# Windowed attention and a gated convolution layer on one core: decoding two weight parts at once, the smaller half of x by TensorE in two units, score bursts next to each other, and a new written-out order

## The chip, the cores and the metric

One core of a Trainium2 chip. The time is that of one execution in microseconds (us) on the device; lower is better. Three runs of the kernel before are given, and one more execution was profiled.

## What is computed

For 8 sequences of 576 positions, 8 heads of 64:

```python
scores = scale * np.matmul(q, k.transpose(0, 1, 3, 2))
mask = (rel >= 0) & (rel < window)            # window 64
attn = softmax of the masked scores
x = attention output, laid out as (batch, seq, 512)
h = np.maximum(x @ w_in, 0.0)                 # 512 -> 1024
conv_out += conv_w[k][None, None, :] * hp[:, k:k + S, :]   # 3 taps along seq
gate = 1.0 / (1.0 + np.exp(-conv_out))
return (h * gate @ w_out)                     # 1024 -> 512
```

The weights come as 64-bit floats, and the kernel decodes them on the chip.

## The kernel before, in words

The 4,608 positions are cut into 12 units of 384. A unit's **attention** has 12 tiles of 64 queries, in bursts: six bursts of two tiles in units 0 and 1, three bursts of four tiles in the others. For a burst TensorE makes the scores (`scores`, L538), VectorE adds the mask and takes the row's extreme (`row_max`, L559), ScalarE takes the exponential (`exps`, L569), and after `guard` and `reciprocal` VectorE or GpSimd normalises (`normalise`, L588). In units 0 and 1 TensorE turns the result (`turn`, L595) and ScalarE or VectorE copies it back (`unturn`, L600); in the others VectorE transposes blocks (L607) and DMAs place them (`place`, L620). `values` (L627) multiplies by v. Its result in PSUM is split in a larger half `xh` (`split_hi`, L632) and the rest `xl` (`split_lo`, L637, always VectorE), so that products of the fp32r kind keep their accuracy.

A unit's **layer** has 8 parts f of 128 hidden columns: `mm1` (L644, 12 matmuls of 384 columns: larger and smaller half of w_in against xh, larger half against xl), `relu` (L670 or L672), for each pair of parts the convolution (`conv_mid` L686 or L688, two `conv_side` L693), `sigmoid` (L697), `gate` (L704), `gate_hi` (L709), `gate_lo` (L714), and `mm2` (L723, 3 matmuls of 512 columns for each part and 128 rows; L728 in the last unit). `result` and the stores follow.

Sixteen weight parts (8 of w_in, 8 of w_out, 512 columns each) are **decoded**: `load_w`, `magnitude` (L438 or L440), `shift` (L444), `sign` (L448), `low` (L451, ScalarE), `add_low` (L455), then `larger` (L471) and `lo` (L475) make the two fp32r halves. Before, only `shift` works on two parts at once.

The PSUM has eight banks. The table gives `scores` a bank for the first head and takes the next one for the second head, so a burst holds two; `mm2` sums in banks 4 to 6, and 0, 1 and 7 go to `mm1` and `values` in turn. TensorE runs `mm1` and `mm2` on fp32r operands and `scores`, `turn` and `values` on fp32 operands.

`plan()` lists the pieces of work, and the string `ORDER` names them one by one: a number is a piece, `/4` its first bank, A, D or P the engine where there is a choice (ScalarE, VectorE, GpSimd), and `F5/0` five `fill` matmuls (L404) on a tile of zeros whose result nobody reads. The instructions are issued in this order, and each engine runs its own in that order.

Of the kernel before, what the change touches and what calls it, by code (L numbers as in the profile page):

```python
# [15 lines left out]
P = 128  # L16
# [21 lines left out]


# [83 lines left out]
def plan():  # L123
# [63 lines left out]
    at("identity")  # L187
    for m in (1, 2):
        at("later_masks", m)
# [60 lines left out]
    224P 240 93P 151A 77/1 231 225 70 152P 75D 232 76 213 78D 226P 468 79 146A 316 73 199 242 215P 233P 206 82  # L250
    F5/2 94/0 147D 241 207P 249 119A 234 120D 123 243P 216 83 121 208/4 250 105/1 122 251 235D 252A 209A 217D
    469 84 128 127 153/7 168 317A 244 200 85 253 245P 96D 318A 106D 107A 254D 3 321 227/5 108 110A 218/6 319
    236/4 155A 111 219A 255/0 326 109 473/2 228A 112 470 246/1 256A 325 367 113 260/7 346 124 169 129 257/0 396
    125P 474 237A 258D 114P 247A 259 261A 475 F3/6 263/1 158A 477 262 266/0 270 320 484/2 327 126D 156/7 264A
    633 322 267A 345 115A 328D 323P 265 170A 268 116P 130A 485 269/1 174 486 157A 161A 131D 179 159 509/2 479
    329D 133/5 171A 324D 634 271A 162 272/0 366 476 172 472 487 173 178 478 290/7 175 273A 480D 163 490 274D 488
    275 136 481 635 160 277A 397 293/1 482P 510 489 471 511 176A 491A 512 278 134/6 177P 492 483 164 132/4 180
    495 137 279 639/2 372 636 165D 369A 135 520 276 166A 330/0 493D 181A 280 167D 513 182P 640 183 508 185 291
    494 281P 186 292D 368A 501 188 641 351 500 184 514 370 507 187 294A 376 502 282A 650/2 371 505 295A 283P
    333/7 504 515 652 499 191A 651 498 190A 797 373 516A 189A 286/6 503 517 518D 374A 285/5 496 348A 375P 519  # L260
    497 288 377 289 298A 332D 523 546 656 674/2 296 506 334A 297 284/4 522 653 299 381/1 378 347A 798 525 300
    356 335D 530 379A 349 301 532 380D 536/0 531 338D 287 355 521 675 528 384/7 383A 302P 537A 526 676 654 524
    538 527 421/1 303D 529 304D 644 799 350 678 336 305 385A 386D 677 306 339 352 533/0 645 340 542/7 655 389D
    337 307 534A 357 643 308 387 800 657A 341 358P 535 309 543D 353P 310 544 424/0 390 642 342D 354D 442/7 422
    658 391 423A 659D 343A 425A 388 646A 539/1 679 344D 445/0 398A 540D 680 647 541 648P 312A 673 681A 392 545/1
    682 359D 683P 649 429A 361/5 660 547A 364 402 393D 661 399A 814/2 638 567 684 311A 662 443 548/1 313A 663
    400 394A 690 401 667 403 668 430 360/4 549A 406 671 363 444A 395D 426A 637 566/1 407 427 404A 428 687 431
    688 569/7 408 192 405D 409A 691 815 446A 410P 686 432 412 664 568A 447D 411 694 450A 433P 816 817 696 362/6
    314 587/0 669 451 588 434D 689 448 414 666 452 590/1 672 435D 695 553D 550A 554 693 417A 415 551 692 449 365
    685 418A 555 413 570A 670 591A 838/2 820 665 437/5 453 839 440 840 416 552 436/4 454D 556 439 419D 818 803/2  # L270
    557D 438/6 961 455D 441 456D 843 697/7 558D 574A 706/1 805 698A 819 459 699 707D 589A 462 821P 559P 808 804
# [12 lines left out]
    767 991 1142/2 917A 885P 992 902A 770 1000 899A 1144 995 788 990 903 769 1143 993 768 989 900 787 999 904
    1166/2 1024 901 918/1 1014 905 1167 966 886A 994 632 1146 887P 771 919D 791 1168 790 1145 906P 789 1172
    1131/2 1170 792 1289 923A 1025/7 793A 795D 1028/0 1133 936/1 907D 1137 908P 1026A 920A 1027 1148 888/4 1029D
    938D 1290 1147 1034/7 1030 1136 1031/1 924 1149P 1171 891 925 1038 1150 1035D 941A 939/0 1059 1132 1151P
    1169 1134 921 909 794A 1291 940D 1032A 890/6 1135 1173D 942 889/5 944D 1138A 892 922 1036 893 926 1165 911
    1139 1033 914 943 1037/0 945 1292 1174 946 1175D 1040/7 1140D 927D 1058/1 1176 928A 1039A 1183 929D 1184
    1061/0 1042D 1060A 1141 947 1152 1041A 948P 932 1157 1306/2 1182 1161 1079/1 1043 1164 1101 949D 1179 1080  # L290
    1308 1187 950D 910 1130 1312 1186 913 1044 1160 912 1307 1163 935 1062A 1045D 1153 1063D 1081A 1330/2 1064
    1185 1066A 1046 953 1311 796 1188 1067 931 1331 934 1047 1180 956 1332 1048 1181 930 1068 1177 952 1065 1159
    933 1155 1069 951 1049P 1158 959A 1295/2 1154 1082/7 1297 1202 1050A 1162 1178 1333 1051D 1453 954 1129
    1084D 1156 1085 1054/6 1336 1070D 1057 1309 1100/0 1296 1083A 1071D 957A 1072P 1334 955 1299 1454 1052/4
    1310 1103/1 1223 1087A 1313P 1335 1088 1102A 1089 1055 958A 1298 1198/7 1104A 1195/0 1455 1199D 1301 1192/1
    1200 1105A 1086 1189/7 1193A 1106 1196A 1075 1314 1300 1108D 1197 1053/5 1302A 1090 1303 1056 1194 1304P
    1190D 1073 1191 1456 1074 1294 1337A 1315P 1305 1078 1076 1201/0 1091P 1316 1329 1327 1320 1109 1092A 1077
    1338 1339D 1204/1 1093P 1340 1352 1470/2 1344 1244 1222/7 1347 1471 1349 1107 1324 1472 1319 1096 1203D
    1224A 1326 1099 1110 1351 1206D 1494/2 1111 1207 1318 1225/7 1208 1474 1343 1496 1348 1112D 1325 1293 1476
    1094 1113D 1317 1226D 1097 1473 1114P 1322 1495 1095 1350 1205D 1243/0 1209A 1230D 1499 1231 1210 1498  # L300
    1459/2 1227D 1475 1228 1246/7 1617 1232 1245A 1328 1477D 1229 1321 1478 1211 1233 960 1115 1479P 1460 1341
# [58 lines left out]
def attention_moe(ctx: ExitStack, tc: tile.TileContext, q, k, v, first, w_in, conv_w, w_out, out):  # L360
# [96 lines left out]
    def part(buf, j):  # L457
        return wx[buf][:, j * DM:(j + 1) * DM]
# [391 lines left out]
```

## Time and profile before

| | |
|---|---|
| time, median of 3 runs | 514.66 us (514.45 to 516.1) |
| the profiled execution | 513.32 us, span 511.5 us |
| TensorE, matmuls | 499.8 us busy (98%) |
| VectorE | 398.7 us (78%) |
| ScalarE | 327.1 us (64%) |
| GpSimd | 169.2 us (33%) |

PE is TensorE's matmuls, PEld its weight loads, DVE is VectorE, ACT ScalarE, POOL GpSimd, SP the queue that issues DMAs. Matmuls overlap, so a matmul's own duration is longer than the step from one to the next, and PE busy is not PE at its peak; the chain view gives the steps. The chain that ended last is 87% TensorE and 9% VectorE by the page.

### The profile page before, as it was taken

The page shows a single profiled execution, that of the slowest core. Times are in us where ns is not written, and L with a number is a line of the kernel's source. Part 1 is how long each engine was busy: PE and PEld are TensorE (multiplying, and loading weights), DVE is VectorE, ACT ScalarE, POOL GpSimd, SP SyncE. Part 2 cuts the span into 40 slices and gives each one's busy share as a digit, 9 for nine tenths or more (in the row PEclk, how much of TensorE's full clock was granted, in tenths as well). Part 3 has the DMA queues.
Part 4 walks back from the last instruction along what each step waited for, and adds up shares of the span by engine and source line. Part 5 has one row for each costly group of instructions (what it writes and reads, how often), then busy time and mean ns, then how long its engine had stood idle before and what let it go on. Part 6 is the DMA issues. An engine that isn't in the chain of part 4 may idle for free.

```text
span 511.5 us, 13953 instructions
## 1 busy us (share of the span) xinstructions
PE 499.8 (98%) x5375; PEld 438.2 (86%) x5375; DVE 398.7 (78%) x1197; ACT 327.1 (64%) x923; POOL 169.2 (33%) x254
## 2 busy tenths in 40 slices
PE   8798999999999999999999999999999999999997
PEld 5587978998888898898888889988889889898996
DVE  5999999997996986597667858887386778846682
ACT  5999999967837863855864874572792675242330
POOL 6766452430441442511332532121344131152020
PEclk9999999999999999999999999999999999999999
DMA  8996635082634533804642613806263303410011
GB/s 326 405 408 216 257 84 146 6 288 85 161 104 114 175 70 105 261 4 125 212 144 70 219 62 112 258 14 197 59 254 110 108 13 113 124 62 33 0 63 62
DMA packets 27570, 71.98 MB, mean 141 GB/s; under 512 B 5744, under 2 KB 14064, under 8 KB 27504
## 3 DMA queue, kind: packets, MB, share of 16 engines
q1 hardware_dynamic: 27216, 69.52, 40.8%
q0 software_dynamic: 288, 1.57, 1.8%
q8 instruction: 42, 0.69, 0.6%
q14 instruction: 24, 0.20, 0.1%
HBM read 48.26 MB, written 11.01 MB: 116 GB/s over the span
## 4 chain that ended last, share of the span: by engine, by line
PE 87%; DVE 9%; POOL 2%; issue 1%; ACT 0%; POOLq 0%
PE bank L723 36%; PE bank L644 36%; PE bank L627 7%; PE bank L538 5%; PE bank L728 3%; DVE s L559 2%; DVE c L693 1%; DVE wx L448 1%; DVE xl L637 1%; POOL s L588 1%; DVE wx L455 1%; DVE s L588 1%; DVE wx L444 0%; ACT s L569 0%; POOL mask L493 0%
## 5 line engine op out<-in xcount | busy, mean ns | idle before, releaser
L644 PE MATMUL bank<-xh,w_in 128*128 128x384 f32 x768 | 197.5, 338 | 0.0
L723 PE MATMUL bank<-w_out,gh 128*128 128x512 f32 x528 | 168.8, 401 | 0.0
L644 PEld LDWEIGHTS bank<-xh,w_in 128*128 128x128 f32 x768 | 138.8, 188 | 7.0
L693 DVE SCALAR_TENSOR_TENSOR c<-hbuf,cw,c 128x386 f32<-128x386 f32 (+1 forms) x192 | 125.0, 674 | 13.8 <-ACT c L686 12.5
L644 PE MATMUL bank<-xl,w_in 128*128 128x384 f32 x384 | 129.0, 336 | 0.9 <-DVE xl L637 0.9
L569 ACT ACTIVATE s<-s,nm 128x96 f32<-128x96 f32 (+2 forms) x288 | 105.2, 368 | 17.1 <-DVE nm L559 16.9
L723 PEld LDWEIGHTS bank<-w_out,gh 128*128 128x128 f32 x528 | 96.0, 188 | 19.0 <-POOL w_out L475 0.2
L723 PE MATMUL bank<-w_out,gl 128*128 128x512 f32 x264 | 104.2, 395 | 0.2 <-DVE gl L714 0.2
L704 POOL TENSOR_TENSOR c<-c,hbuf 128x386 f32<-128x386 f32 (+5 forms) x39 | 44.8, 1166 | 110.4 <-ACT c L697 110.4
L559 DVE CUSTOM_DVE_ANT_0 s<-bank,mask 128x96 f32<-128x96 f32 (+2 forms) x288 | 56.6, 255 | 29.3 <-PE bank L538 25.1
L644 PEld LDWEIGHTS bank<-xl,w_in 128*128 128x128 f32 x384 | 72.1, 188 | 1.3 <-DVE xl L637 1.3
L697 ACT ACTIVATE c<-c 128x772 f32<-128x772 f32 (+1 forms) x48 | 40.6, 849 | 35.6 <-DVE c L693 35.3
L714 POOL TENSOR_TENSOR gl<-c,gh 128x768 fp32r<-128x768 f32 (+1 forms) x22 | 42.5, 1930 | 57.5 <-DVE gh L709 32.0
L723 PEld LDWEIGHTS bank<-w_out,gl 128*128 128x128 f32 x264 | 49.5, 188 | 12.2 <-DVE gl L714 0.6
L569 ACT ACTIVATION_READ_ACCUMULATOR s<-s,nm 128x1 f32 x288 | 54.6, 189 | 0.0
L670 ACT ACTIVATE hbuf<-bank 128x384 f32<-128x384 f32 x55 | 26.0, 484 | 44.1 <-PE bank L644 41.8
L588 POOL TENSOR_TENSOR s<-s,r 128x768 f32<-128x768 f32 (+1 forms) x22 | 30.1, 1376 | 62.0 <-DVE r L581 57.8
L686 ACT ACTIVATE c<-hbuf,cw 128x386 f32<-128x386 f32 (+1 forms) x57 | 34.1, 613 | 17.2 <-POOL gl L714 6.4
L627 PEld LDWEIGHTS bank<-ub,v 128*64 128x64 f32 x1152 | 35.6, 138 | 8.2 <-issue 4.4
L538 PEld LDWEIGHTS bank<-qk 64*32 64x32 f32 (+1 forms) x2112 | 29.6, 110 | 13.3 <-issue 6.6
L627 PE MATMUL bank<-ub,v 128*64 128x64 f32 x1152 | 38.7, 224 | 1.3 <-ACT ub L600 1.3
L538 PE MATMUL bank<-qk 64*32 64x96 f32 (+2 forms) x2112 | 38.2, 253 | 1.0 <-DMA qk<-in_first_dram 0.6
(78 smaller groups left out, 538.0 us busy)
## 6 DMA issues: line engine op xcount, KB each, us to landing
v<-in_v_dram SPq DMA_DIRECT2D x24, 768.0 KB, 5.5
ub<-T SPq DMA_DIRECT2D x240, 48.0 KB, 2.2
qk<-in_k_dram SPq DMA_DIRECT2D x20, 448.0 KB, 4.6
out_dram<-ot SPq DMA_DIRECT2D x11, 768.0 KB, 4.7
qk<-in_q_dram SPq DMA_DIRECT2D x20, 384.0 KB, 5.5
raw_in<-in_w_in_dram SPq DMA_DIRECT2D x8, 512.0 KB, 6.3
raw_out<-in_w_out_dram SPq DMA_DIRECT2D x8, 512.0 KB, 7.7
qk<-in_first_dram SPq DMA_DIRECT2D x12, 320.0 KB, 4.6
```

Source lines behind the costliest of these rows:

```text
L538: nc.tensor.matmul(banks[bank[h]][r:r + rows, i * P + o:i * P + k], qq[hs, s:s + rows], kk[hs, s + o:s + k], start=True, stop=True)
L559: nc.vector.tensor_tensor_reduce(out=ss[n // NB][:, n % NB, h, o:k], in0=banks[bank[h]][:, i * P + o:i * P + k], in1=mask[m][:, o:k], scal ...
L569: nc.scalar.activation(x, x, AF.Exp, bias=small(nms, (n,))[:, h:h + 1], scale=-1.0, accum_out=small(sms, (n,))[:, h:h + 1])
L588: engine[on].tensor_tensor(sv, sv, small(rs, ns).unsqueeze(2).broadcast_to([P, 2 * len(ns), k]), ALU.mult)
L627: nc.tensor.matmul(banks[bank[0]][h * D:(h + 1) * D, t * W:(t + 1) * W], vs[:, c, t, h], ub[g][:, 2 * p:2 * p + 2, 2 * t + h], start=True, ...
L644: nc.tensor.matmul(banks[bank[0]][:, :NX], w[:, a, c], y[x][:, c], start=(c == 0 and j == 0), stop=(c == NC - 1 and j == 2))
L686: nc.scalar.activation(c, h, AF.Copy, scale=w)
L693: nc.vector.scalar_tensor_tensor(c, h, w, c, op0=ALU.mult, op1=ALU.add)
L697: nc.scalar.activation(both(u, j), both(u, j), AF.Sigmoid)
L704: engine[on].tensor_tensor(c[:, :, a:a + n], c[:, :, a + o:a + o + n], h[:, :, 1 + a + o:1 + a + o + n], ALU.mult)
L714: engine[on].tensor_tensor(gls[j % 3][:, :, :n], cs[j % 2][:, :, :n], ghs[j % 3][:, :, :n].bitcast(F32), ALU.subtract)
L723: nc.tensor.matmul(banks[bank[0]], x, wts["out", f][:, w], start=(start and i == 0), stop=(stop and i == 2))
```

## The change

- All of a decode step's instructions now take a whole pair of parts (1,024 columns) where the pair belongs together, which is the case for 14 of the 16 parts; the raw tile and the weight tile of a pair are one tile each.
- In units 1 and 2 the smaller half of x is made by TensorE: `less` adds minus `xh` to the result of `values` in the same bank (one matmul of 384 columns against a negated identity, built once by `minus`), and `split_rest` copies the rest out on ScalarE (5 times) or VectorE (3 times). `split_lo` stays in the other units.
- `values` starts its bank only with its first tile.
- `ORDER` is another one, with 12 `fill` matmuls in place of 23. It also moves work between engines.

```diff
+BY_DIFFERENCE = (1, 2)
...
-        for j, f in enumerate(fs):
-            at("magnitude", key, f, buf, j)
-        at("shift", key, fs, buf)
-        for j, f in enumerate(fs):
-            for fn in ("sign", "low", "add_low", "larger", "lo"):
-                at(fn, key, f, buf, j)
+        for fn in ("magnitude", "shift", "sign", "low", "add_low", "larger", "lo"):
+            at(fn, key, fs, buf)
...
             at("values", u, c, bank=bank)
             at("split_hi", u, c, bank=bank)
-            at("split_lo", u, c, bank=bank)
+            if u in BY_DIFFERENCE:
+                at("less", u, c, bank=bank)
+                at("split_rest", u, c, bank=bank)
+            else:
+                at("split_lo", u, c, bank=bank)
...
-    2 6 8 5 97 4 86 7 13 41 9 0 F5/0 31/2 50/4 382 95 32 195 1 22/6 80 331 154 51 33 98D 23 F3/0 12/2 99 34 100
+    0 7 98 5 9 143 351 8 1 6 42 2 312 10 14 F4/0 32/2 33 178 102 87 99D 34 F3/0 13/4 100 101 51/6 103 176 15 133
...
-    def part(buf, j):
-        return wx[buf][:, j * DM:(j + 1) * DM]
+    def part(buf, fs):
+        return wx[buf][:, :len(fs) * DM]
...
+        w = wts[key, fs] = pool.tile([P, 2, len(fs) * DM], F32R, name=f"w_{key}{fs[0]}", tag=f"{key}{fs[0]}")
+        for j, f in enumerate(fs):
+            wts[key, f] = w[:, :, j * DM:(j + 1) * DM]
+        copy(on)(w[:, 0], part(buf, fs))
...
+    def minus():
+        nc.scalar.activation(negated, ident, AF.Copy, scale=-1.0)
...
-                                 ub[g][:, 2 * p:2 * p + 2, 2 * t + h], start=True, stop=True)
+                                 ub[g][:, 2 * p:2 * p + 2, 2 * t + h], start=(t == 0), stop=(t == NT - 1))
...
+    def less(u, c, bank):
+        nc.tensor.matmul(banks[bank[0]][:, :NX], negated, xh[x_of(u)][:, c], start=False, stop=True,
+                         skip_group_check=True)
...
+    def split_rest(u, c, on, bank):
+        copy(on)(xl[x_of(u)][:, c], banks[bank[0]][:, :NX])
```

Three places of the order. **GpSimd at the start**: mask_75 is the mask that the scores of units 0 and 1 need, mask_76 a mask of the later units. Before, from the program's first mask on:

```order
L489 MEMSET mask_76 128x128
L493 ISA
L493 AFFINE_SELECT mask_76<-mask_76 32x96
L495 AFFINE_SELECT mask_76<-mask_76 32x96
...
L551 MEMSET s_81 128x2x64
L551 MEMSET s_82 128x2x64
L489 MEMSET mask_75 128x128
L493 AFFINE_SELECT mask_75<-mask_75 64x128
L495 AFFINE_SELECT mask_75<-mask_75 64x128
L493 AFFINE_SELECT mask_75<-mask_75 64x128
L495 AFFINE_SELECT mask_75<-mask_75 64x128
```

Now:

```order
L497 MEMSET mask_75 128x128
L501 ISA
L501 AFFINE_SELECT mask_75<-mask_75 64x128
L503 AFFINE_SELECT mask_75<-mask_75 64x128
L501 AFFINE_SELECT mask_75<-mask_75 64x128
L503 AFFINE_SELECT mask_75<-mask_75 64x128
L674 MEMSET hbuf 128x2x2
```

The mask that is needed first is now made first; the ten instructions for the other mask and the two blanks no longer stand ahead of it.

**TensorE at the values of unit 1** (ub_61 and ub_62 hold the two groups of turned weights; before, bank_104 is bank 0, now bank_105 is). Before:

```order
L595 MATMUL bank_105<-ident,s_83 128x128 x4
L627 MATMUL bank_111<-ub_61,v 64x64 x12
L627 MATMUL bank_104<-ub_61,v 64x64 x12
L404 MATMUL bank_110<-spare 128x512 x3
L627 MATMUL bank_105<-ub_62,v 64x64 x12
L627 MATMUL bank_104<-ub_62,v 64x64 x12
L538 MATMUL bank_106<-qk 32x96
```

Now, with `less` on L653 (negated is the negated identity):

```order
L639 MATMUL bank_106<-ub_61,v 64x64 x12
L639 MATMUL bank_105<-ub_61,v 64x64 x12
L607 MATMUL bank_111<-ident,s_83 128x128 x4
L653 MATMUL bank_106<-xh_64,negated 128x384
L665 MATMUL bank_112<-xh_63,w_in_459 128x384 x2
...
L639 MATMUL bank_106<-ub_62,v 64x64 x12
L639 MATMUL bank_112<-ub_62,v 64x64 x12
L653 MATMUL bank_105<-xh_64,negated 128x384
L653 MATMUL bank_106<-xh_64,negated 128x384
L550 MATMUL bank_107<-qk 32x96
```

Each bank of values gets one matmul more; three fills are gone; and an `mm1` stands between the two halves of the values.

**TensorE at the scores of unit 7**, now: two bursts stand next to each other, the first in banks 2 and 3 (bank_107, bank_108), the second in banks 0 and 1 (bank_105, bank_106). Before, the three bursts of this unit stand apart, with `mm1` and `mm2` between them, all three in banks 2 and 3.

```order
L744 MATMUL bank_110<-w_out_1376,gl_99 128x512
L550 MATMUL bank_107<-qk 32x96
L550 MATMUL bank_108<-qk 32x96
...
L550 MATMUL bank_107<-qk 32x96
L550 MATMUL bank_108<-qk 32x96
L550 MATMUL bank_105<-qk 32x96
L550 MATMUL bank_106<-qk 32x96
...
L550 MATMUL bank_105<-qk 32x96
L550 MATMUL bank_106<-qk 32x96
L744 MATMUL bank_110<-w_out_1376,gh_96 128x512 x2
```

This is so in units 7 to 11; over the whole order, TensorE's stretches of fp32 work (scores, turns, values) between fp32r work go from 54 to 48.

## Rows read from the trace of the kernel before

**Rows 1.** The page: TensorE's busy time, and its busy tenths in 40 slices of the span.

```profile
PE 499.8 (98%) x5375; PEld 438.2 (86%) x5375; DVE 398.7 (78%) x1197; ACT 327.1 (64%) x923; POOL 169.2 (33%) x254
...
PE   8798999999999999999999999999999999999997
```

**Rows 2.** Stretches of the span (us): length, busy time of each engine with its instructions, then TensorE's granted clock (1.00 is the full one), the DMA engines' share, and GB/s.

```profile
6.00:9.00 3.00, 2.89 (x37) 1.84 (x30) 2.97 (x23) 2.77 (x13) 0.49 (x7) 1.00 1.02 402
...
30.00:45.00 15.00, 13.57 (x277) 12.11 (x278) 14.93 (x52) 14.91 (x35) 9.78 (x21) 1.00 0.76 304
45.00:70.00 25.00, 24.84 (x326) 21.42 (x307) 24.90 (x86) 24.04 (x72) 12.23 (x13) 1.00 0.57 202
70.00:98.00 28.00, 28.00 (x280) 25.01 (x281) 27.29 (x79) 27.87 (x85) 9.08 (x11) 1.00 0.36 100
98.00:300.00 202.00, 202.00 (x2242) 176.56 (x2242) 160.74 (x478) 132.78 (x373) 64.29 (x84) 1.00 0.46 139
300.00:508.00 208.00, 207.93 (x1937) 185.90 (x1935) 146.29 (x380) 103.29 (x263) 52.57 (x73) 1.00 0.30 95
```

**Rows 3.** What TensorE's matmuls waited for in the first 70 us: total us, times, the longest.

```profile
PE bank L595 <- POOL s L588: 3.1, 4, 1.2
...
PE bank L627 <- ACT ub L600: 1.3, 1, 1.3
PE bank L644 <- DVE xl L637: 0.9, 1, 0.9
...
PE bank L723 <- DVE gl L714: 0.2, 1, 0.2
```

**Rows 4.** The chain that ended last, from 60 to 80 us: start, us, what.

```profile
64.15 0.88 DVE gl L714
65.03 0.04 issue
65.08 3.97 PE bank L723 x16
```

**Rows 5.** In order of time, the start: GpSimd's masks, VectorE's first work on scores, TensorE's first scores. Start, duration, engine, line, what, and idle time before it.

```profile
0.73 0.20 POOL L489 MEMSET mask<- 128x128 f32 x1 [0.29 <-POOLq L839]
...
3.84 0.20 POOL L489 MEMSET mask<- 128x128 f32 x1
...
3.88 2.84 PE L538 MATMUL bank<-qk 64*64 64x128 f32 x48
...
5.16 0.29 POOL L495 TENSOR_SCALAR_AFFINE_SELECT mask<-mask 64x128 f32<-64x128 f32 x1
...
5.48 0.29 DVE L559 CUSTOM_DVE_ANT_0 s<-bank,mask 128x128 f32<-128x128 f32 x1 [4.09 <-POOL mask L495]
```

**Rows 6.** Groups by line and shape in the first 70 us: instructions, busy us, mean ns of one, idle time before.

```profile
L448 DVE SCALAR_TENSOR_TENSOR wx<-raw_in,wx 128x512 uint32<-128x512 uint32 x8 | 5.4, 691 | 0.1
L451 ACT ACTIVATE raw_in<-raw_in 128x512 uint32<-128x512 uint32 x7 | 4.8, 680 | 0.0
L637 DVE TENSOR_TENSOR xl<-bank,xh 128x384 fp32r<-128x384 f32 x8 | 4.2, 549 | 0.1
L475 POOL TENSOR_TENSOR w_in<-wx,w_in 128x512 fp32r<-128x512 f32 x3 | 4.2, 1418 | 0.1
L444 DVE TENSOR_SCALAR wx<-wx 128x1024 uint32<-128x1024 uint32 x5 | 3.8, 751 | 0.1
L632 ACT CAST xh<-bank 128x384 fp32r<-128x384 f32 x5 | 2.2, 475 | 0.0
L475 DVE TENSOR_TENSOR w_in<-wx,w_in 128x512 fp32r<-128x512 f32 x3 | 2.0, 681 | 0.0
L714 POOL TENSOR_TENSOR gl<-c,gh 128x768 fp32r<-128x768 f32 x1 | 1.9, 1859 | 0.0
L714 DVE TENSOR_TENSOR gl<-c,gh 128x768 fp32r<-128x768 f32 x1 | 0.9, 949 | 0.0
L444 DVE TENSOR_SCALAR wx<-wx 128x512 uint32<-128x512 uint32 x2 | 0.8, 418 | 0.0
```

**Rows 7.** In order of time, VectorE and GpSimd between 56 and 60 us (columns as in the rows 5).

```profile
56.18 0.57 DVE L693 SCALAR_TENSOR_TENSOR c<-hbuf,cw,c 128x386 f32<-128x386 f32 x1
...
58.04 1.29 POOL L475 TENSOR_TENSOR w_out<-wx,w_out 128x512 fp32r<-128x512 f32 x1
...
58.09 1.67 DVE L693 SCALAR_TENSOR_TENSOR c<-hbuf,cw,c 128x386 f32<-128x386 f32 x1
```

**Rows 8.** The chain that ended last, later pieces: start, us, what, number of matmuls.

```profile
76.00 0.90 PE bank L723 x3
...
102.58 2.31 PE bank L644 x12
...
112.53 2.11 PE bank L644 x12
114.64 0.71 PE bank L723 x3
...
126.70 1.55 PE bank L627 x48
...
259.12 3.02 PE bank L627 x96
```

**Rows 9.** In order of time, two groups of fills on TensorE.

```profile
1.45 2.50 PE L404 MATMUL bank<-spare 128*128 128x512 f32 x5 [1.45 <-DVE spare L760]
...
40.48 0.96 PE L404 MATMUL bank<-spare 128*128 128x512 f32 x3
```

More of the change, by code (lines that the diff above doesn't have):

```diff
@@ L250 @@
[L250 to L259, printed above, removed]
@@ new lines @@
+    944 845A 844A 955 752A 846 959 848A 753P 715 991 863A 963 716 987 735 847 966 864/7 849 962 980 956 1109/2
+    865D 986 869A 882/0 965 1111 960 866D 850 964 1110 851 958 885/1 870 985 867 983 868 961 871 733 932 872 957
+    1133/2 1113 967 873P 736 1135 988 754 984 1134 734 852P 990 1112 737 886A 884A 1098/2 1139 1026 1005 738
+    1136 904 1100 1256 1138 903/7 853D 1099 1114 854P 755 905A 1115 890D 756 874D 1257 757 891 875P 759 760A
+    1104 758 855/4 1137 858 1116A 1101 1117 1118P 998/1 1258 1103 1001/0 762A 999D 908A 1000 992/7 887D 888
@@ new lines @@
+    1227 1482 1338 1606 1477 1229 1244D 1355A 1626 1452 1605 1590/2 1627 1425 1607 1356/7 1480 1339 1630 1473
+    1608D 1342 1479 1245D 1459 1225 1358D 1357A 1455 1343 1230 1361D 1472 1362 1247 1359 1424 1374/0 1609 1453
+    1591 1344P 1748 1457 1481 1228 1363 1345A 1248 1497 1360 1250 1346P 1376D 1364 1377/1 1631 1365P 1749 1246
+    1476 1628 1251 1253A 1379D 1395/7 1396 1592 1254A 1518 1593 1610D 1629 1380 1249 1632D 1633 1378D 1634P
+    1349/6 1252A 1596 1348/5 1255 1381 1750 1484/0 1382A 1383 1487/1 1485A 1595 1486 1347/4 1488D 1594 1352
@@ L345 @@
+    2070D 2051 2071D 2031 2056 2030 2049 2050 2054 2073 2077 2055 2075 2079 2074 2088 2086 2082D 2053 2089 2083
+    2078 2087 2072 2084D 2076 2085 2080A 2081
 """
@@ L379, in attention_moe @@
     ident = pool.tile([P, P], F32, name="ident")
+    negated = pool.tile([P, P], F32R, name="negated")
     qk = pool.tile([P, FIRST], F32, name="qk")
@@ L424, in load_w @@
     def load_w(key, f):
-        raws[key, f] = pool.tile([P, DM, 2], U32, name=f"raw_{key}{f}", tag=f"{key}{f}")
-        nc.sync.dma_start(raws[key, f].rearrange("p e two -> p (e two)"), src[key][f].bitcast(U32))
+        fs = next(fs for k, fs in DECODE if k == key and f in fs)
+        if (key, fs) not in raws:
+            raws[key, fs] = pool.tile([P, len(fs) * DM, 2], U32, name=f"raw_{key}{fs[0]}", tag=f"{key}{fs[0]}")
+        a = fs.index(f) * DM
+        nc.sync.dma_start(raws[key, fs][:, a:a + DM].rearrange("p e two -> p (e two)"), src[key][f].bitcast(U32))
     @work
@@ L455, in to_add_low @@
         nc.vector.tensor_tensor(xu, xu, lw, ALU.add)
-    def part(buf, j):
-        return wx[buf][:, j * DM:(j + 1) * DM]
-    fn["magnitude"] = lambda key, f, buf, j, on: to_magnitude(part(buf, j), raws[key, f][..., 1], on)
-    fn["sign"] = lambda key, f, buf, j: to_sign(part(buf, j), raws[key, f][..., 1])
-    fn["low"] = lambda key, f, buf, j: to_low(raws[key, f][..., 0])
-    fn["add_low"] = lambda key, f, buf, j: to_add_low(part(buf, j), raws[key, f][..., 0])
+    def part(buf, fs):
+        return wx[buf][:, :len(fs) * DM]
+    fn["magnitude"] = lambda key, fs, buf, on: to_magnitude(part(buf, fs), raws[key, fs][..., 1], on)
+    fn["sign"] = lambda key, fs, buf: to_sign(part(buf, fs), raws[key, fs][..., 1])
+    fn["low"] = lambda key, fs, buf: to_low(raws[key, fs][..., 0])
+    fn["add_low"] = lambda key, fs, buf: to_add_low(part(buf, fs), raws[key, fs][..., 0])
     def copy(on):
@@ L468, in larger, with lo @@
     @work
-    def larger(key, f, buf, j, on):
-        wts[key, f] = pool.tile([P, 2, DM], F32R, name=f"w_{key}{f}", tag=f"{key}{f}")
-        copy(on)(wts[key, f][:, 0], part(buf, j))
+    def larger(key, fs, buf, on):
+        w = wts[key, fs] = pool.tile([P, 2, len(fs) * DM], F32R, name=f"w_{key}{fs[0]}", tag=f"{key}{fs[0]}")
+        for j, f in enumerate(fs):
+            wts[key, f] = w[:, :, j * DM:(j + 1) * DM]
+        copy(on)(w[:, 0], part(buf, fs))
     @work
-    def lo(key, f, buf, j, on):
-        engine[on].tensor_tensor(wts[key, f][:, 1], part(buf, j), wts[key, f][:, 0].bitcast(F32), ALU.subtract)
+    def lo(key, fs, buf, on):
+        w = wts[key, fs]
+        engine[on].tensor_tensor(w[:, 1], part(buf, fs), w[:, 0].bitcast(F32), ALU.subtract)
     @work
@@ L506, in identity @@
         make_identity(nc, ident)
+    @work
+    def minus():
+        nc.scalar.activation(negated, ident, AF.Copy, scale=-1.0)
     @work
@@ L637, in split_lo @@
         nc.vector.tensor_tensor(xl[x][:, c], banks[bank[0]][:, :NX], xh[x][:, c].bitcast(F32), ALU.subtract)
+    @work
+    def less(u, c, bank):
+        nc.tensor.matmul(banks[bank[0]][:, :NX], negated, xh[x_of(u)][:, c], start=False, stop=True,
+                         skip_group_check=True)
+    @work
+    def split_rest(u, c, on, bank):
+        copy(on)(xl[x_of(u)][:, c], banks[bank[0]][:, :NX])
     @work
```

175 lines of the change are left out of this document (86 added, 89 removed).

## The prediction

> **What bounds the kernel now.** I read the page first: TensorE is busy 98% of the span, and only the first tenth of it shows gaps [rows 1]. Then the stretches: from 70 us to 508 us its matmuls fill 437.93 of 438 us at the full granted clock, and the view of what they waited for has no entry after 70 us [rows 2]. Up to 70 us it is different. VectorE is busy 14.93 of 15 us and 24.90 of 25 us, ScalarE 14.91 and 24.04, while TensorE stands in some places for normalised scores (3.1 us), a copied bank (1.3), the smaller half of x (0.9) and a last time for the smaller half of the gate (0.2) [rows 2, 3]. That last one is where the chain leaves VectorE: gate_lo ends and TensorE starts at 65.08 us and is never released by anyone again [rows 4]. So the time is: when TensorE becomes dense, plus the work that it has left then. A microsecond is won in the first 70 us only through VectorE and ScalarE, and later only by less work on TensorE.
>
> **The change, part by part.** The sum is made against the profiled execution, 513.32 us, which lies 1.34 us under the median of 514.66 us; the difference found is then taken from the median. I counted each engine's work in both orders up to the same piece of TensorE work, at the step from one instruction to the next: on VectorE a row's mean less about 0.08 us of overlap, on ScalarE less about 0.1.
>
> *Start.* VectorE's first row_max waits 4.09 us for the mask, which ends at 5.45 us, since another mask is made first, from 0.73 to 3.84 us [rows 5]. With its own mask first (five instructions, 1.6 us from the second memset to the end), the mask is ready near 2.4 us. Late next are the scores: TensorE starts them at 3.88 us, 48 in 2.84 us, so 16 of a burst take 0.95 us and VectorE can start at 4.9 instead of 5.48 us. Gain 0.6 us; between 0 (the second burst's data now land behind a weight part) and 1.3 (if ScalarE wins as well).
>
> *Up to the fourth mm1 of unit 0* (29 us of TensorE work, 45 us in the trace) VectorE has 38.1 us to do in place of 38.3, ScalarE 37.3 in place of 37.2, GpSimd 25.3 in place of 28.5. Pairing is worth little: two halves of 512 columns are 836 ns, one of 1,024 is 751, so 0.08 us for each of the 22 or so instructions saved on VectorE and some 0.13 on ScalarE, estimated the same way [rows 6]. And part of the pairs is not yet due. I take 0.2 us gained, between 1.0 gained and 0.5 lost.
>
> *less.* Eight matmuls of 384 columns at 2.11 / 12 = 0.176 us [rows 8] are 1.4 us on TensorE. Four belong to unit 1, where TensorE waits anyway (the 1.3 us for the bank copied by ScalarE stand right between the two halves of these values) [rows 3]; I let them cost 0.1. The four of unit 2 lie where it is dense and cost 0.7. Sum 0.8; bounds 0.7 and 1.4. split_lo in return frees VectorE of eight times 0.47 us [rows 6]; three copies of the same length come back there, and five of 0.37 go to ScalarE. Both are in the loads here and below.
>
> *Between 29 and 76 us of TensorE work* the new order shifts work off GpSimd. By 76 us VectorE has lo (+2.1 us, now as pairs), two more gates (+1.9), two more gate_lo (+1.7), two more normalise (+1.5) and magnitudes (+1.1), and loses split_lo (-2.4 net of copies), a few conv_mid (-1.0) and relu (-0.9), and unturn, sign and add_low (-1.4), with small things of +0.4: +3.0. ScalarE gets +0.9, GpSimd -12.8 (lo 4.0, gate 3.6, gate_lo 3.6, normalise 1.0). VectorE had no idle time there, so this is the danger. What eases it is that a VectorE instruction with two inputs in SBUF waits out a GpSimd one: the convolution that takes 0.57 us took 1.67 when a GpSimd lo of 1.29 began 0.05 us earlier [rows 7]. Between 45 and 98 us VectorE is busy 52.2 us [rows 2], and its instructions there at their usual steps are some 49.3 us by my count, so some 2.9 us are such waiting; with half of GpSimd's work I expect half of that back, 1.4. So VectorE is later by 3.0 - 0.8 (the gains above) - 1.4 = 0.8 us. TensorE itself is later by 0.8 + 0.2 (less, and one more switch, below) - 0.8 = 0.2, so VectorE loses 0.6 against it, and by how much its results lay ready the trace does not tell. I take 0.2 us lost; bounds 0 and 3.
>
> *Switches.* Behind scores or values the next mm1 takes 2.31 us in place of 2.11, the next three mm2 matmuls 0.90 in place of 0.71, and two separate pairs of values take 2 x 1.55 where four in one go take 3.02 [rows 8]. A stretch of fp32 work thus costs 0.20 to 0.28 us beyond its matmuls; I take 0.24. After 80 us of TensorE work the order has 32 of them in place of 38, by bursts next to each other and by values in threes: 1.4 us gained (1.2 to 1.7). In the middle there is one more: 0.2 lost.
>
> *Fills.* Eleven fewer. The ones removed stand in waits, so I cost them at nothing; that cover is the wait itself, and if it is gone a fill less is a gain. [...]
>
> The *end* (results and stores of the last unit) keeps its shape, cost nothing. Sum: -0.6 - 0.2 + 0.8 + 0.2 - 1.4 + 0.2 = **-1.0 us**: 512.3 for the profiled execution, **513.7 us** as a median. Some 0.3% (1.5 us) is what a measurement can tell from no change here, so this is inside it, on the fast side.
>
> **Rivals.** *(1) More of it counts.* The start gives 1.0, the first stage 0.5, less costs 0.7, VectorE is no later, switches give 1.7 and take 0.2: -2.3 us, 512.4. For it speaks that TensorE has no wait after 70 us even though VectorE is just as full up to 98 us [rows 2], so results lie ready. *(2) VectorE becomes the bound between 65 and 120 us (slower).* If GpSimd's relief does not come and the results were only just ready, the 3.0 us count in full, and less 1.2: -0.6 - 0.2 + 1.2 + 3.0 + 0.2 - 1.4 = +2.2, 516.9. It decides the sign once TensorE waits more than 1.2 us for gate_lo, xl or relu there. The 0.2 us wait at 65 us [rows 3, 4] says that this slack can be gone. *(3) The bursts do not stay next to each other in effect.* Two bursts hold four banks, and the third needs the first two back; if VectorE is late with the row_max, TensorE waits in five units, up to 0.5 us each: +1.5, 516.2. Against it: a second burst (0.93 us) and two mm2 groups (1.4 us) stand between in the closest place, and VectorE has idle time in that part (160.74 of 202 us) [rows 2]. [...]
>
> **How the numbers follow.** Forecast 0.45; rival 1 0.35; rival 2 0.12; rival 3 0.04; rival 4 0.04. The forecast's own bounds run from about -1.9 to +0.7 by terms that do not all fall to one side. The range takes in rival 1 with some 0.5 us below it and most of the way to rival 2: 511.9 to 516.4. Faster by over 0.3% (under 513.1): rival 1 and a little of the forecast, 0.37. Within: most of the forecast and a part of the rivals at the border, 0.44. Slower: rivals 2 to 4, 0.19.
>
> **What would show it.** Right: VectorE's first row_max near 4.9 us; the fourth mm1 of unit 0 starts at 44 to 45 us; no matmul wait after 70 us beyond 0.5 us; three mm2 matmuls behind two bursts still 0.90, with six such stretches fewer; less near 0.18 us each. Wrong: TensorE waiting for VectorE between 65 and 120 us (rival 2), waits of scores for nm at units 7 to 11 (rival 3), a granted clock under 1.00 (rival 4), or a start of the dense part later than 66 us.

## The result and the profile after

520.0 us as a median (518.13 to 520.15), against 514.62 for the kernel before on the same chip: 1.0083 times as long, 95% interval 1.0061 to 1.0105. The forecast was 513.7 and its range ended at 516.4; the change makes the kernel slower by 5.4 us. The profiled execution took 520.15 us against 513.32 before, 6.8 us more; their spans, 518.1 and 511.5 us, are 6.6 apart. (The execution profiled before lay 1.3 us under its median, which is why these are more than 5.4.)

The page shows where to look. TensorE's busy time grew by only 1.0 us, its tenths show a new dent in the 22nd slice (272 to 285 us), and the granted clock, shown full in all slices before, is lower in the third and in that 22nd:

```profile
PE 500.8 (97%) x5372; PEld 441.5 (85%) x5372; DVE 399.9 (77%) x1186; ACT 321.8 (62%) x905; POOL 156.7 (30%) x238
...
PE   8679999999999999999997999999999999999997
...
PEclk9989999999999999999998999999999999999999
...
q8 instruction: 42, 0.69, 0.6%
```

What the matmuls waited for, over the whole run (before, the main rows are those of [rows 3]):

```profile
PE bank L607 <- POOL s L600: 5.1, 2, 3.5
PE bank L550 <- issue: 3.0, 1, 3.0
PE bank L639 <- ACT ub L612: 1.8, 2, 1.0
PE bank L406 <- DVE spare L781: 1.5, 1, 1.5
PE bank L550 <- DMA qk<-in_first_dram: 1.1, 4, 0.3
PE bank L607 <- DVE s L600: 0.9, 2, 0.6
PE bank L639 <- DVE nm L571: 0.5, 1, 0.5
```

Two rows are new: one wait of 3.5 us for GpSimd's normalise, and one of 3.0 us for "issue", that is for nothing that the profile knows. The first begins at 28 us. The second stands in the chain at 278.86 us, in the middle of a burst of scores; it is called the standstill from here on:

```profile
274.85 1.67 PE bank L550 x99
276.52 1.59 PE bank L744 x6
278.12 0.74 PE bank L550 x43
278.86 3.00 issue
281.86 0.66 PE bank L550 x18
282.52 1.57 PE bank L744 x3
284.09 2.77 PE bank L665 x12
```

Behind it three mm2 matmuls take 1.57 us and an mm1 2.77, where 0.71 (0.90 behind a burst) and 2.11 are usual [rows 8]. The stretches that answer to [rows 2]:

```profile
30.00:45.00 15.00, 12.96 (x170) 12.18 (x171) 14.04 (x42) 11.62 (x32) 10.95 (x15) 0.89 0.82 328
45.00:70.00 25.00, 25.00 (x347) 22.31 (x346) 24.93 (x66) 24.82 (x59) 7.45 (x10) 1.00 0.60 215
70.00:98.00 28.00, 28.00 (x316) 23.88 (x314) 27.72 (x86) 27.60 (x90) 4.74 (x7) 1.00 0.45 135
98.00:300.00 202.00, 199.00 (x2207) 175.13 (x2207) 155.93 (x472) 129.06 (x360) 62.99 (x88) 0.99 0.45 133
300.00:508.00 208.00, 208.00 (x1979) 186.37 (x1978) 151.91 (x395) 103.79 (x268) 52.33 (x70) 1.00 0.31 96
```

From 45 us on TensorE is full but for the 3.0 us. From 30 to 45 it is less full than before (12.96 against 13.57 us), and VectorE, which had next to no idle time there before, now has 1.0 us.

To place the loss I worked out from the matmul records how much TensorE is behind: the start of a matmul less the usual steps of all matmuls ahead of it (0.174 us for 384 columns, 0.233 for 512, 0.109 for a turn, 0.033 for one of values, 0.015 to 0.017 of scores; fills count as nothing). In us, at these times of the span:

```
                        20 us   50 us   80 us  270 us  300 us     end
before                  15.48   22.30   23.66   27.30   28.06   30.48
after                   15.61   25.25   25.86   29.36   34.34   35.79
e3_mask_early           15.75   22.90   23.51   27.02   31.46   32.99
e5_unit8_apart          15.48   25.28   25.85   29.31   29.87   31.45
e6_data_later           15.62   25.33   25.87   29.34   30.12   31.63
e7_mask_early_unit8...  15.39   22.58   23.15   26.48   27.05   28.67
```

Before to after: +0.13 up to 20 us, +2.82 from there to 50, -0.89 to 270, +4.22 in the 30 us of the standstill, -0.97 behind it; the eight `less` matmuls add 1.39 us of steps. Together this is +6.7, the difference of the spans (6.6) but for rounding. So there are two losses, 2.8 and 4.2 us, and a gain of some 1.9 us outside them, where the forecast had one.

### The profile page after: what moved, and what is told of

Its sections match the earlier page's. It is cut to its first block, busy times and chain, and to the rows that moved or that the text cites. A ratio compares the mean times of both kernels' runs of the same rounds, so it can differ in the third digit from the quotient of the medians.

```text
span 518.1 us, 13893 instructions
## 1 busy us (share of the span) xinstructions
PE 500.8 (97%) x5372; PEld 441.5 (85%) x5372; DVE 399.9 (77%) x1186; ACT 321.8 (62%) x905; POOL 156.7 (30%) x238
## 3 DMA queue, kind: packets, MB, share of 16 engines
q0 software_dynamic: 288, 1.57, 1.7%
## 4 chain that ended last, share of the span: by engine, by line
PE 93%; DMA 2%; issue 1%; DVE 1%; ACT 1%; POOL 0%; SPq 0%
PE bank L665 40%; PE bank L744 37%; PE bank L639 7%; PE bank L550 6%; PE bank L749 3%; DMA qk<-in_first_dram 2%; PE bank L607 1%; PE bank L653 0%; ACT s L581 0%; DVE s L571 0%; DVE wx L460 0%; POOL s L600 0%; POOL w_in L478 0%; SPq L411 0%; DVE w_in L483 0%
## 5 line engine op out<-in xcount | busy, mean ns | idle before, releaser
L665 PEld LDWEIGHTS bank<-xh,w_in 128*128 128x128 f32 x768 | 140.6, 190 | 6.2
L714 DVE SCALAR_TENSOR_TENSOR c<-hbuf,cw,c 128x386 f32<-128x386 f32 (+1 forms) x192 | 120.6, 655 | 14.7 <-ACT c L707 13.0
L735 POOL TENSOR_TENSOR gl<-c,gh 128x768 fp32r<-128x768 f32 x21 | 39.8, 1894 | 92.6 <-ACT gh L730 56.1
L725 POOL TENSOR_TENSOR c<-c,hbuf 128x386 f32<-128x386 f32 (+5 forms) x31 | 37.8, 1237 | 79.1 <-ACT c L718 79.1
L707 ACT ACTIVATE c<-hbuf,cw 128x386 f32<-128x386 f32 (+1 forms) x59 | 35.4, 614 | 30.9 <-DVE hbuf L693 24.1
L639 PEld LDWEIGHTS bank<-ub,v 128*64 128x64 f32 x1152 | 35.7, 138 | 9.1 <-issue 5.3
L693 DVE TENSOR_SCALAR hbuf<-bank 128x384 f32<-128x384 f32 x40 | 21.8, 549 | 26.9 <-PE bank L665 25.7
```

What stands on the lines that cost most here:

```text
L639: nc.tensor.matmul(banks[bank[0]][h * D:(h + 1) * D, t * W:(t + 1) * W], vs[:, c, t, h], ub[g][:, 2 * p:2 * p + 2, 2 * t + h], start=(t == ...
L665: nc.tensor.matmul(banks[bank[0]][:, :NX], w[:, a, c], y[x][:, c], start=(c == 0 and j == 0), stop=(c == NC - 1 and j == 2))
L707: nc.scalar.activation(c, h, AF.Copy, scale=w)
L714: nc.vector.scalar_tensor_tensor(c, h, w, c, op0=ALU.mult, op1=ALU.add)
L725: engine[on].tensor_tensor(c[:, :, a:a + n], c[:, :, a + o:a + o + n], h[:, :, 1 + a + o:1 + a + o + n], ALU.mult)
L735: engine[on].tensor_tensor(gls[j % 3][:, :, :n], cs[j % 2][:, :, :n], ghs[j % 3][:, :, :n].bitcast(F32), ALU.subtract)
```

## The experiments

All times are medians; the kernel before ran beside them (514.64, 514.73 and 515.19 us in the three sets). In these kernels' traces the line numbers are two lower, since the table of numbers wraps differently (in the second experiment two higher). In the diffs a token is a step of the table, a number and behind a slash its bank: 4 and 3 are the masks of later units, 1437/2 and 1426/2 the first and third burst of unit 8, 1171/0 an mm1, 1260 the load of v, 927 the store, 1584 a load of k.

**First: the third burst moved, at the wrong unit.** Theory A: TensorE runs out of instructions, since scores and their weight loads use them up at some 140 per us (64 of each in the 0.93 us of a burst).

```diff
-1262/2
 1097 1298 1148 1046/7
+1262/2
```

> The changed kernel with one edit: the third burst of unit 7 (scores(7,0)) stands behind mm1(5,4) instead of in front of it, so that 24 slow instructions (2.1 us) stand between the double burst and it. Theory A (TensorE ran out of instructions at 278.6 us: 384 scores and their weight loads are eaten faster than the next instruction transfer lands, at 280.4): the 3.0 us standstill and the half rate behind it (1.5 us) go, 515 to 516 us. Rival B (the third burst waits for VectorE to free banks 2 and 3): mm1 takes the place of up to 2.1 us of that wait, 517 to 518, and some wait stays in front of the burst. Rival C (something at that time, not that place, such as a transfer that blocks): the standstill stays near 278 us, 520.

Measured: 520.02 us, and the standstill is still there, 278.61 to 281.38 us. It looks like rival C and is a mistake of mine: the burst at 278 us belongs to unit 8, as counting the matmul records along TensorE's order shows; unit 7's bursts run at 242 to 246 us. The run says only that an edit there changes nothing here.

**Second: 160 more TensorE instructions, 250 us earlier.**

```diff
+    def tiny(n, bank):
+        for _ in range(n):
+            nc.tensor.matmul(banks[bank][:32, :32], spare[:64, :32], spare[:64, :32], start=True, stop=True)
...
-30/7
+T50/7 30/7
...
-72/1
+T30/1 72/1
```

> The changed kernel with 80 very small matmuls (64x32 by 64x32, 160 instructions with their weight loads) put into two waits of TensorE at 15 and 24 us; all else stays. Theory A: instruction transfers come every 256 instructions, so the one that was late now falls due 160 instructions earlier in the program, in mm2 and mm1, and lands before the double burst of unit 7; no standstill there, 515 to 516.5 us if the small matmuls stay inside their waits; another, shorter standstill could turn up where the due point now meets scores (near 409 us at the earliest by the count). Rivals B and C: the standstill at 278 us is as it was, 520 to 521.

Measured: 515.31 us (515.07 to 516.31), no wait for issue anywhere; the chain goes through the same burst without a stop:

```profile
277.79 0.97 PE bank L552 x56
278.76 0.89 PE bank L746 x3
```

Work, banks, transfers and order round unit 8 are those of the changed kernel; only the place at which an instruction transfer falls due has moved. Rival B is out, and so is C as the whole cause: the data transfers are there at the same time and alone stop nothing. (That they have a part in it, the sixth experiment shows.)

The trace also has the instruction transfers themselves. On the queue q8 there are 42 of 16,384 bytes, 0.69 MB by the page. TensorE has 10,869 instructions in the trace (10,744 matmuls and weight loads, and 125 others, nearly all on semaphores). That makes 259 for a transfer and 63 bytes for each; I estimate 256 and 64. With its 160 more instructions this kernel has 43 transfers. Counting how many of all these had begun when transfer n (from 0) started, less 256 n, shows how far TensorE has come:

```
kernel                       n  starts   took  begun at start  begun when landed  standstill
before                      24  273.66   1.15       231              245             none
before, latest of all        1   25.25   1.09       372              413             none
after                       24  279.42   0.99       449              449             3.0 us
e4_fills_in_wait            24  279.52   1.00       449              449             3.0 us
e6_data_later               24  276.29   1.41       343              355             0.26 us
e5_unit8_apart              24  273.60   2.07       195              216             none
e2_more_instructions...     25  279.08   0.95       393              401             none
```

In slow stretches a transfer starts at 152 to 170, so I estimate that it becomes due about there. In the changed kernel and those of the first, third, fourth, sixth and eleventh experiments TensorE stopped at 449, the same place in the 256. So it has some 280 to 300 instructions from the due point on. Whether they last depends on what they are (the two bursts are 256 instructions in 1.7 us) and on when the transfer lands. TensorE went on 1.26 to 1.45 us after the landing (280.41 to 281.86 in the changed kernel, 277.70 to 279.14 in the sixth).

**Third: the second mask made at the start.** Theory D on the 3.5 us at 28 us.

```diff
-42 2 312 10 14
+42 2 312 10 14 4
...
-212/4 4 136
+212/4 136
```

> The changed kernel with one edit: the mask of the sequences' first blocks (17 GpSimd instructions, 20.85 to 26.9 us) is made right behind the blanks at the start, where GpSimd is idle from 3.6 to 8.5 us. Theory D (GpSimd's mask work delays the casts, lo and normalise that turn(1) of unit 1 and the first mm1 wait for): normalise ends 2 to 3 us earlier, the wait of 3.5 us at 28 us falls under 1.5 us, and the whole takes 517 to 518 us. Rival E (the transfers of q and k at the start, or VectorE, set the pace): under 0.5 us gained, 519.5 to 520.

Measured: 517.29 us, 2.7 less; 2.35 of it is there by 50 us in the table above. Rival E is out. GpSimd in the changed kernel:

```profile
20.85 0.21 POOL L497 MEMSET mask<- 128x128 f32 x1
...
21.79 1.20 POOL L503 TENSOR_SCALAR_AFFINE_SELECT mask<-mask 32x96 f32<-32x96 f32 x1
...
23.23 1.11 POOL L501 TENSOR_SCALAR_AFFINE_SELECT mask<-mask 32x96 f32<-32x96 f32 x1
...
27.20 1.04 POOL L478 CAST w_in<-wx 128x1024 fp32r<-128x1024 f32 x1
...
28.63 2.35 POOL L483 TENSOR_TENSOR w_in<-wx,w_in 128x1024 fp32r<-128x1024 f32 x1
30.94 2.04 POOL L600 TENSOR_TENSOR s<-s,r 128x512 f32<-128x512 f32 x2
```

and in this one:

```profile
24.37 1.43 POOL L476 CAST w_in<-wx 128x1024 fp32r<-128x1024 f32 x1 [2.54 <-DMA qk<-in_k_dram]
...
26.19 2.38 POOL L481 TENSOR_TENSOR w_in<-wx,w_in 128x1024 fp32r<-128x1024 f32 x1
28.52 2.04 POOL L598 TENSOR_TENSOR s<-s,r 128x512 f32<-128x512 f32 x2
```

The chain is mask, cast, lo, normalise, and then TensorE, which takes the turn at 32.03 in the one and at 29.63 us in the other:

```profile
27.84 0.73 PE L406 MATMUL bank<-spare 128*128 128x512 f32 x2
32.03 0.66 PE L607 MATMUL bank<-ident,s 128*128 128x128 f32 x4 [3.45 <-POOL s L600]
```

The mask takes 6.0 us there and 3.8 at the start: a select of 0.26 us takes up to 1.2 beside these VectorE instructions, which have two inputs in SBUF:

```profile
21.64 1.23 DVE L453 SCALAR_TENSOR_TENSOR wx<-raw_in,wx 128x1024 uint32<-128x1024 uint32 x1
...
23.00 1.23 DVE L460 CUSTOM_DVE_ANT_0 wx<-raw_in,wx 128x2048 uint16<-128x2048 uint16 x1
```

Whether the two inputs are what matters was not tried apart.

**Fourth: fills through the wait, for the clock.**

```diff
-F2/2 201/0
+F18/2 201/0
```

> The changed kernel with 18 fills instead of 2 in the wait from 27.8 to 32.0 us (32 instructions more). Theory F (mm1(0,0) runs at half rate, 32.9 to 36.1 us, because TensorE stood before it): full rate there, 1.5 us less, if the fills end by 32.0; the standstill at 278 us stays, since 32 instructions more leave the due point at the start of the double burst: 518.5 us. Rival G (the half rate comes from something else, such as the load of the whole chip): no gain, 520. Before the change the same mm1 stood at half rate too (27.3 to 30.9 us), so this says nothing on the difference between the two kernels.

Measured: 521.46 us, no gain. The last sentence of the expectation is wrong: before the change the clock in 26 to 34 us was 1.00, and the 3.6 us of that mm1 hold a wait of 0.94 us for the smaller half of x [rows 3]. The fills did what they were put there for, mm1(0,0) starts at 32.56 and runs at full rate (clock 1.00 from 30 to 35 us, where the changed kernel has 0.50 from 33 to 36); but 1.4 us of wait for the normalise of a later turn stand in its place:

```profile
27.85 4.39 PE L404 MATMUL bank<-spare 128*128 128x512 f32 x18
...
38.42 1.00 PE L548 MATMUL bank<-qk 64*32 64x96 f32 x64
40.81 0.66 PE L605 MATMUL bank<-ident,s 128*128 128x128 f32 x4 [1.39 <-POOL s L598]
```

By 50 us it is as late as the changed kernel (25.42 and 25.25 us behind). So the slow mm1 there lies under the chain of GpSimd and costs nothing. The standstill stayed, from 278.80 us, as expected for a shift of only 32 instructions. That this kernel is 1.5 us slower than the changed one comes from behind it: the clock is 0.50 until 288 us, so that the next mm1 takes 3.80 us in place of 2.77.

**Fifth: the right unit.**

```diff
-1045 1077 1314 1171/0
+1045 1437/2 1077 1314 1171/0
...
-1437/2 1286
+1286
```

> The changed kernel with one edit, at the place that stood still: of unit 8's double burst the first (scores(8,1)) stands behind mm2(5,3,2) and in front of mm1(6,1), so that 24 slow instructions stand inside the run of bursts (the edit of the first experiment was 33 us too early, in unit 7). Theory A (instructions run out): by the time that the late transfer has landed (5.3 us after its due point) TensorE has used about 250 instructions since that point and not 299, so the standstill (3.0 us) and the half rate behind it (1.5 us) are gone; one switch more, +0.2: 515.5 to 516.5 us. Rival B (the third burst waits for banks): no gain, since the third burst stands as close to the second as before; 519 to 520.

Measured: 515.74 us; no standstill, the clock 1.00 throughout 270 to 286 us. Theory A holds, and rival B fails here too, since the third burst stands as close to the second as it did. But the standstill went in another way than the expectation says: with the first burst earlier the transfer starts at 273.60 us, at 195 in place of 449 (table above), while the DMA engines move 127 GB/s (273 to 274 us). They reach 400 only at 277 us. So it was not late here, and this run alone doesn't show what slow instructions inside the run of bursts would do.

**Sixth: the data moved out of the way, TensorE's order untouched.**

```diff
-1260 927 1059D
+1059D
...
-1584
+1584 1260 927
```

> The changed kernel with the load of v of unit 7's first half (768 KB, issued at 272.6 us) and the store of unit 4 (768 KB, 273.2) issued behind the next load of k, near 285 us; TensorE's order is as it was. Theory A in its full form (the instructions run out because their transfer starts 4.3 us after its due point, and it starts late since the data transfers fill all 16 engines from 277 to 280 us): the transfer starts within 2 us of its due point and no standstill is left, 515 to 516.5 us. Theory A without the data (the transfer is late by itself whenever scores run): the standstill stays, 520.

Measured: 515.54 us. In the changed kernel the DMA engines (the last column but one) are full while the transfer is due, and the clock falls behind the standstill:

```profile
277.00:278.00 1.00, 1.00 (x5) 0.56 (x3) 1.00 (x13) 0.78 (x1) 0.35 (x3) 1.00 0.97 399
278.00:279.00 1.00, 0.86 (x47) 0.60 (x47) 1.00 (x11) 0.98 (x2) 0.87 (x1) 1.00 1.02 421
279.00:280.00 1.00, 0.00 (x0) 0.00 (x0) 1.00 (x1) 0.99 (x4) 1.00 (x2) 1.00 0.94 316
...
282.00:284.00 2.00, 2.00 (x22) 1.43 (x15) 0.00 (x0) 2.00 (x11) 0.00 (x0) 0.51 0.25 65
```

With the load of v and the store later:

```profile
277.00:278.00 1.00, 1.00 (x5) 0.56 (x3) 1.00 (x13) 0.79 (x1) 0.35 (x3) 1.00 0.14 34
278.00:279.00 1.00, 0.88 (x47) 0.60 (x47) 1.00 (x10) 0.98 (x2) 0.88 (x1) 1.00 0.20 51
```

The transfer now starts at 276.29 instead of 279.42 us, and TensorE still stops at the same instruction, but for 0.26 us:

```profile
278.07 0.81 PE L548 MATMUL bank<-qk 64*32 64x96 f32 x46
279.14 0.49 PE L548 MATMUL bank<-qk 64*32 64x96 f32 x18 [0.26 <-issue]
```

So the long standstill needs the data transfers; without them 0.26 us are left. The run of short instructions is the other half: in the second experiment a transfer is late too (279.08 us, at 393), but it falls due at another place in the run, and nothing stops. A small miss: a remnant of the standstill is left, which I had not expected.

**Seventh: both.** The diffs of the third and the fifth in one kernel.

> Both edits together: the second mask at the start (as in the third experiment, which gave 2.7 us) and unit 8's double burst apart. If the two losses are independent, they add up: 520.0 - 2.7 - 4.3 = 513.0 us, which is the forecast of the prediction (513.7) without the two losses that it did not see, and within 0.3% of the kernel before. If a third loss hides behind them, 514.5 or more.

Measured: 513.09 us (512.91 to 513.37), 0.9966 of the kernel before (0.9955 to 0.9978). The losses add up, nothing hides behind them, and without them the change is a gain of 1.6 us.

**Eighth and ninth: the third mask too.** In the seventh kernel token 3 is moved from behind 188D to behind 222 (21 us), or to the start.

```diff
-222
+222 3
...
-188D 3 95/7
+188D 95/7
```

> As the one before, and the third mask (8 selects, 6.3 us of GpSimd's time from 30.5 to 36.8 us there, which held up the normalise that the last turn of unit 1 waited 1.3 us for) is made at 21 us, where GpSimd waits 2.5 us. If GpSimd still sets the pace in the first 40 us: 1.0 to 1.3 us less than the one before, 512 us. If VectorE and ScalarE do by then: the same as the one before.

Measured: 514.9 us, 1.8 more than the seventh. GpSimd's idle 2.5 us at 21 us are no room for it:

```profile
21.60 1.02 POOL L499 TENSOR_SCALAR_AFFINE_SELECT mask<-mask 32x96 f32<-32x96 f32 x1
22.69 1.29 POOL L501 TENSOR_SCALAR_AFFINE_SELECT mask<-mask 32x96 f32<-32x96 f32 x1
...
26.33 1.04 POOL L476 CAST w_in<-wx 128x1024 fp32r<-128x1024 f32 x1
...
30.07 2.05 POOL L598 TENSOR_TENSOR s<-s,r 128x512 f32<-128x512 f32 x2
```

The cast is back at 26.33 us, and the wait for the turn back at 3.0. A miss of the forecast, and theory D the other way round.

```diff
-14 4
+14 4 3
...
-188D 3 95/7
+188D 95/7
```

> The second mask at the start and unit 8's double burst apart (513.09 us so far), and the third mask right behind the second one, at 7 us in GpSimd's idle time, instead of at 30.5 us. At 21 us the third mask took 5.0 us and pushed the first cast of a pair from 24.4 to 26.3 us. At the start nothing of VectorE's with two inputs in SBUF runs beside it until 6.9 us, so its 2.7 us should push GpSimd's first cast only from 8.95 to 9.8. If GpSimd sets the pace at 37 us (a wait of 1.3 us for normalise): 512.0 us. If that wait only goes over to VectorE: 513. If the later first cast costs: up to 513.9.

Measured: 514.77 us, a miss again. The masks end only at 10.9 us:

```profile
10.95 0.61 POOL L476 CAST w_in<-wx 128x512 fp32r<-128x512 f32 x1
...
13.31 1.04 POOL L598 TENSOR_TENSOR s<-s,r 128x512 f32<-128x512 f32 x1
```

The first normalise had begun at 10.88 in the changed kernel; now the first turn waits 2.9 us for it, and the clock is 0.50 from 15 to 20 us. The third mask is best left where the change has it.

**Tenth: what a pair of bursts is worth.** The seventh kernel with units 7, 9, 10 and 11 apart as well:

```diff
-898
+1273/2 898
...
-1226
+1601/2 1226
...
-1393
+1754/2 1393
...
-1558
+1929/2 1558
```

(and the four tokens taken out at their old places)

> The kernel with the second mask at the start and unit 8's double burst apart (513.09 us), with the double bursts of units 7, 9, 10 and 11 apart too: the first burst of each stands one mm2 earlier. By the price of a switch in the prediction (0.24 us) this costs 4 times 0.24, so 514.05 us. If the pairs of bursts bring nothing of what the prediction says, 513.1.

Measured: 514.54 us, 1.45 more: 0.36 us for each instead of the 0.24 expected. So the gain that the change makes for is real, and larger than its price in the prediction.

**Eleventh: the changed kernel's TensorE order, without both losses.** The diffs of the third and the sixth.

> The changed kernel with the second mask at the start and with the load of v and the store beside unit 8 issued later: TensorE's order is exactly that of the changed kernel. The two edits alone gave 517.29 and 515.54 us from 520.0; together 520.0 - 2.7 - 4.5 = 512.8 us. That is 0.2 to 0.3 less than with unit 8's bursts apart (513.09), one switch. If what was seen as the standstill depends on the place after all, 515 or more.

Measured: 513.15 us, ratio 0.9963 (0.9950 to 0.9976). It is within 0.1 us of the seventh, so the 0.2 to 0.3 us expected for unit 8's pair do not show. A remnant of the standstill takes as much: from the matmul that starts at 276.17 to the next at 276.47 us, at 449 again. Otherwise this is the change as it was meant, and again faster than the kernel before.

## Why the prediction was wrong

*Start*, -0.6: nothing came of it (at 20 us TensorE is 0.1 us later than before). The first row_max starts at 5.17 us, before 5.48 but not at the 4.9 of the forecast, since its sixteen scores take 1.13 us and not 0.95. The second burst then waits for q and k behind a weight part until 6.79 us, the lower bound that the text named:

```profile
3.88 1.13 PE L550 MATMUL bank<-qk 64*64 64x128 f32 x16 [0.35 <-DMA qk<-in_first_dram]
...
5.17 0.29 DVE L571 CUSTOM_DVE_ANT_0 s<-bank,mask 128x128 f32<-128x128 f32 x1 [3.78 <-PE bank L550]
...
6.79 0.92 PE L550 MATMUL bank<-qk 64*64 64x64 f32 x16 [0.21 <-DMA qk<-in_first_dram]
```

*Up to the fourth mm1 of unit 0*, -0.2: **this is the first step that failed**; it measured +2.8, and that mm1 starts at 48.96 us, not at 44 to 45 (before, at 45.21). It is not the engines' loads: in the first 45 us VectorE is busy 37.98 us in place of 39.47, ScalarE 35.76 in place of 38.63, and both now stand idle in between. (Whether the counts up to that mm1 are right in themselves is not shown; by then the engines have done other work as well.) A sum does not say what stands ahead of what. GpSimd has less to do (29.16 us in place of 31.00) and is late all the same, by the order of its masks. Before, one of the two later masks was made from 0.73 to 3.84 us [rows 5], when only the first row_max waited for GpSimd, and the other from 35.7 to 41.4. Now the second is made from 20.9 to 26.9 us and the first from 32.9 to 39.2: 12.3 us of masks in this stage in place of 5.7, and 6.0 of them right ahead of a cast, a lo and a normalise that TensorE waits for. The text named the gain of making the needed mask first and never asked where the others went. The third and the eighth experiment show it both ways. The third brings back 2.35 us of the 2.8 by 50 us; what the rest is stays open.

*less*, 0.8: eight at 0.174 us each, 1.4. The four of unit 1, costed at 0.1 because TensorE waits there, stand at 43 to 49 us, where it no longer waits. The upper bound was right. In the chain one of them takes 0.18 us, as forecast, and the three others of unit 1, right behind values or scores, 0.92 together, since a switch falls on them.

*29 to 76 us of TensorE work*, +0.2: right. From 50 to 100 us TensorE falls behind by 1.66 us after and by 1.75 before, and no matmul waits for VectorE there. Rival 2 did not happen.

*Switches*, -1.4 and +0.2: right in kind, and more in size. Outside the two losses the changed kernel gains 1.9 us behind 50 us, the 0.2 us for the last wait of [rows 3] at 65 us among it; that leaves 1.7 for the 1.2 of the forecast. By the tenth experiment a switch is worth 0.36 us and not 0.24.

*Fills*, 0: right as far as was tried; the fourth experiment put sixteen back in one wait, and by 50 us nothing was gained. But a clock of 1.00 at the start, as [rows 2] have it from 6 us on, is not what was measured: the traces have no record of the clock before 7.25 us (before the change) and 12.39 us (now), and the views show 1.00 where there is none. The matmuls say otherwise. In the changed kernel 64 scores from 7.99 us take 3.70 us, 0.058 each, where 48 at 20.91 us in the third experiment take 1.44, 0.030 each; before, three fills from 8.48 us on take 0.96 us, as those at 40 us [rows 9] do. So TensorE ran at about half its rate for longer than before. By 20 us it is 0.1 us later in all; whether the missing fills are the reason was not tried.

**The second failed step is one that is missing**: the supply of instructions, 4.2 us. The text listed what the third of three bursts could wait for (row_max, rival 3) and gave 0.04 to a falling clock (rival 4), and both look like what happened: the third burst stands, and the clock falls to 0.51 of the full one from 282 to 284 us (in the sixth experiment's first rows). But the burst waited for instructions, and the clock fell where TensorE had stood for 3.0 us: where nothing or 0.26 us of standstill is left, in the second, fifth and sixth experiments, it is 1.00 there. That it could fall by itself, for want of fills, was my estimate, and no run shows it. Of the 4.2 us, 3.0 are the standstill and 1.2 the lower clock behind it.

The sum with the measured terms: +0.1 + 2.8 + 1.4 - 1.9 + 4.2 = +6.6 us, against a forecast of -1.0. (They are parts of one measured difference and so add up by themselves; what shows the two losses are the runs without them.)

## What to carry to other kernels

Sums of work per engine bound a stage from below only; for what is moved, follow the queue it was moved into, instruction by instruction, up to the one that somebody waits for, even on an engine that is busy 30% of the time. A run of short instructions is a load on the instruction transfers (here 256 in 1.7 us, by my estimate a whole transfer's worth): count instructions per us, not only columns, and look for large loads and stores issued just ahead of the run. A wait for "issue" in the middle of a run of equal instructions can be a late instruction transfer; here one of 3.0 us went away when harmless instructions were added far ahead of it, and the transfers are in the trace to be counted.

## What the runs showed of the hardware

That an instruction transfer competes with data at all I had not expected: at one place it started 3.1 us later (279.42 in place of 276.29 us) for two transfers of 768 KB issued at 272.6 and 273.2. Between its landing and TensorE's next instruction lie 1.26 to 1.45 us in the kernels that stopped. A select of GpSimd of 32x96 takes 0.26 us alone and up to 1.32 beside VectorE (at 37.53 us in the changed kernel). Two things were not tried apart: which of the two data transfers held the instructions up, and why no standstill came in the other units with pairs, whose due points lay elsewhere in the bursts.
